# Loads of the first weights placed between those of k and v, and v in rows of 1 KB, in an attention-and-softplus kernel

## Chip, cores, metric

One core of one Trainium2 chip. The time is that of the device in microseconds (us), over whole executions of one program. The engines are PE (TensorE, matrix products), DVE (VectorE), ACT (ScalarE), POOL (GpSimd), and SP, which here only issues transfers (DMA). The granted clock is the share of its full speed that PE was given, as the profile recorded it; 1.00 is full.

## The reference, cut to what matters

```python
kv  = np.einsum('bhsd,bhse->bhde', k, v)              # b = 8, h = 8, s = 576, d = e = 64
out = np.einsum('bhsd,bhde->bhse', q, kv)
x   = out / np.sqrt(np.mean(out*out, -1, keepdims=True) + 1e-06) * g_norm   # -> (4608, 512)
h   = x @ w_in                                        # 512 -> 2048
y   = (np.maximum(h, 0) + np.log1p(np.exp(-np.abs(h)))) @ w_out             # 2048 -> 512
```

The two weights arrive as 64-bit floats.

## The kernel before

A plan written in the kernel sorts all tasks by a position number, engine by engine, and the tasks are then emitted in that order. Every engine works through its own list in order. What matters here is the start: the weights of 16 chunks (w_in and w_out each) are fetched and converted from 64-bit words into three 32-bit parts, four chunks of them for the first phase; k and v of a batch give kv, q times kv gives rows, these are normalised and turned, and then the large products begin: h from x and w_in, the sums from softplus(h) and w_out.

The conversion of a weight is a chain between ACT and DVE, in tiles of which there is one or two:

```python
f  = add("SP", 450, fetch, when, pos, [raw], size=2300, behind=int(pos) - 3)
a1 = add("ACT", 670, square, [f], pos, [sq], [raw])
a2 = add("ACT", 670, low, [f], pos, [lf], [raw])
d1 = add("DVE", 430, high1, [f], pos, [t], [raw])
d2 = add("DVE", 690, high2, [d1], pos, [], [raw])
d3 = add("DVE", 690, mask, [d2, a1], pos, [], [sq])
over_done.append(add("ACT", 910, beyond, [a1], pos, [junk], [sq, junk]))   # the overflow check
d4 = add("DVE", 430, power, [d3], pos, [p])
d5 = add("DVE", 690, rest, [d4, a2], pos, [], [lf])
ready = add("DVE", 690, total, [d3, d5], pos, [w], [t, p])
# ... then divide(): high (ACT), low (DVE), low_up (ACT), two products (PE), third (ACT)
```

k, v and q come by tiles of 128 tokens and 8 heads, so one row of a transfer is the 64 floats of a token and a head, 256 B:

```python
for b, r0, n, s0 in parts(t):
    nc.sync.dma_start(out=x[r0:r0 + n], in_=src[b, :, s0:s0 + n].rearrange("h s d -> s h d"))
# kv of a batch, for each of its tiles: four products of two heads, 128x128x128
nc.tensor.matmul(kv[:, p], lhsT=pairs(k_slots[t].tile[r0:r0 + n], p),
                 rhs=pairs(v_slots[t].tile[r0:r0 + n], p), ...)
```

and the weights' place in the plan is one number for both fetching and converting:

```python
if c < 4:
    pos = -18.0 + 0.8 * j if j < 2 else -13 + 1.6 * j     # j = 2 * chunk + (1 for w_out)
# ... later chunks at later places ...
fetched.append(weight(j, pos, ()))
```

## Time and profile before

| | before |
|---|---|
| time, median of 6 executions | 949.6 us (948.8 to 950.8) |
| profiled execution (948.7 us, as fast as the fastest of the six) | span 946.9 us, mean granted PE clock 0.996 |
| PE busy | 920.4 us, 97% |
| PE idle up to 66 us / 66 to 940 us / at the end | 21.4 / 0 / 5.2 us |

How to read it: PE runs without a gap from 66 us to 940 us, so only the first 66 us are open to a change that leaves PE's work as it is. The prediction shows the views that say so. Beside those, the page's part on transfers, with the packets by size and the time that the queue's packets took as a share of all 16 DMA engines' span:

```profile
DMA packets 172738, 135.63 MB, mean 143 GB/s; under 512 B 118656, under 2 KB 126848, under 8 KB 172672
...
q1 hardware_dynamic: 172512, 134.77, 48.3%
```

Over two thirds of all packets have under 512 B; nearly all of these are the 256 B rows of k, v and q (36 tiles of 1024 rows for each, 110592).

### The profile page before, as it was taken

Reading aid. Unit: us, or ns where it says so; the run is one execution under the profiler, and the core shown is the slowest. Engines: PE = TensorE matmul, PEld = TensorE weight load, DVE = VectorE, ACT = ScalarE, POOL = GpSimd, SP = SyncE. Lnnn points to the kernel's source line nnn. Section 1 sums busy time; section 2 is a strip of 40 time slices with the busy share of each in tenths; the row PEclk is TensorE's granted clock in tenths of the full one; section 3 lists DMA queues with packets and bytes.
Section 4 is the critical chain, followed back from the end, with each engine's and each line's share of the span. In section 5 each row is a group of like instructions: output and inputs, shape, how many; then the busy total and the mean of one; then the engine's idle time right before and its main releaser. Section 6 shows DMA issues by size and latency. Waiting matters only on the chain.

```text
span 946.9 us, 13479 instructions
## 1 busy us (share of the span) xinstructions
PE 920.4 (97%) x4978; PEld 834.2 (88%) x4978; DVE 596.5 (63%) x1043; ACT 443.7 (47%) x871; POOL 66.6 (7%) x42
## 2 busy tenths in 40 slices
PE   4889999999999999999999999999999999999997
PEld 3779999999999999998999999999999999999996
DVE  4997776867767566777676666485554544544552
ACT  4886665656656554454344334274233233233231
POOL 0213221222222000000000000000000000000000
PEclk9999999999999999999999999999999999999999
DMA  9996878777764433333333343442322332322321
GB/s 225 252 201 168 245 200 228 204 224 193 209 187 170 167 123 123 127 108 127 125 137 116 126 149 101 145 145 100 101 100 100 100 101 101 100 76 85 100 74 67
DMA packets 172738, 135.63 MB, mean 143 GB/s; under 512 B 118656, under 2 KB 126848, under 8 KB 172672
## 3 DMA queue, kind: packets, MB, share of 16 engines
q1 hardware_dynamic: 172512, 134.77, 48.3%
q8 instruction: 39, 0.64, 0.3%
q14 instruction: 27, 0.22, 0.1%
q10 hardware_dynamic: 160, 0.00, 0.0%
HBM read 93.85 MB, written 40.89 MB: 142 GB/s over the span
## 4 chain that ended last, share of the span: by engine, by line
PE 94%; DVE 2%; DMA 1%; ACT 1%; issue 0%; SPq 0%; POOL 0%; DVEq 0%; POOLq 0%
PE s L530 42%; PE h L523 42%; PE o L435 4%; PE o L461 3%; PE tp L455 2%; PE tp L477 1%; DMA kvt<-in_v_dram 1%; DVE w L289 0%; DVE t L273 0%; DVE t L268 0%; DVE p L286 0%; DMA out_dram<-qT 0%; PE s L461 0%; POOL r L469 0%; DVE r L465 0%
## 5 line engine op out<-in xcount | busy, mean ns | idle before, releaser
L530 PE MATMUL s<-w,gv 128*128 128x512 f32 x1728 | 438.5, 396 | 0.0
L523 PE MATMUL h<-xv,w 128*128 128x384 f32 x2304 | 435.9, 337 | 0.1
L523 PEld LDWEIGHTS h<-xv,w 128*128 128x128 f32 x2304 | 406.0, 188 | 14.6 <-ACT g L543 0.4
L530 PEld LDWEIGHTS s<-w,gv 128*128 128x128 f32 x1728 | 318.1, 188 | 57.9 <-issue 0.5
L543 ACT ACTIVATE g<-h 128x384 f32<-128x384 f32 x192 | 94.5, 492 | 417.0 <-PE h L523 408.7
L534 DVE TENSOR_TENSOR gv<-g,gv 128x384 fp32r<-128x384 f32 x192 | 106.7, 556 | 183.1 <-ACT gv L545 182.8
L538 DVE SCALAR_TENSOR_TENSOR gv<-gv 128x384 fp32r<-128x384 f32 x192 | 106.9, 557 | 5.2
L545 ACT ACTIVATE gv<-g 128x384 fp32r<-128x384 f32 x192 | 100.8, 525 | 6.1 <-PE s L530 1.4
L398 DVE TENSOR_TENSOR xv<-xt,xv 128x512 fp32r<-128x512 f32 x102 | 70.2, 688 | 45.0 <-ACT xv L395 44.8
L469 POOL TENSOR_TENSOR r<-r,half 128x8 f32<-128x8 f32 x36 | 65.9, 1832 | 238.6 <-DVE r L466 235.7
L401 DVE SCALAR_TENSOR_TENSOR xv<-xv 128x512 fp32r<-128x512 f32 x108 | 74.6, 691 | 2.9
L395 ACT ACTIVATE xv<-xt 128x512 fp32r<-128x512 f32 x102 | 62.9, 623 | 2.0 <-DMA xt<-x 2.0
L435 PE MATMUL o<-kvt,kvt 128*128 128x128 f32 (+1 forms) x320 | 45.7, 292 | 11.4 <-DMA kvt<-in_v_dram 11.4
L435 PEld LDWEIGHTS o<-kvt,kvt 128*128 128x128 f32 (+1 forms) x320 | 42.9, 204 | 14.9 <-issue 11.4
L570 DVE SCALAR_TENSOR_TENSOR qT<-s,scale,kvt 128x512 f32<-128x512 f32 x36 | 26.9, 749 | 37.3 <-PE s L530 29.8
L570 DVE SCALAR_TENSOR_TENSOR qT<-s,kvt 128x512 f32<-128x512 f32 x36 | 24.6, 687 | 25.5 <-PE s L530 18.1
L461 PE MATMUL o<-kv_diag,qT 128*128 128x128 f32 (+1 forms) x296 | 37.0, 276 | 0.0
L461 PEld LDWEIGHTS o<-kv_diag,qT 128*128 128x128 f32 (+1 forms) x296 | 34.6, 179 | 1.5 <-issue 0.3
L465 DVE TENSOR_REDUCE r<-x 128x8 f32<-128x512 f32 x36 | 24.6, 684 | 15.0 <-ACT x L485 14.6
L491 ACT ACTIVATE xg<-tp,g_col 128x512 f32<-128x512 f32 x36 | 24.7, 686 | 12.8 <-PE tp L477 12.3
L472 DVE TENSOR_TENSOR x<-o,r 128x512 f32<-128x512 f32 x33 | 22.7, 688 | 6.7 <-POOL r L469 6.1
L480 ACT COPY qT<-tp 128x512 f32<-128x512 f32 x36 | 21.0, 582 | 12.5 <-PE tp L455 12.2
(61 smaller groups left out, 453.5 us busy)
## 6 DMA issues: line engine op xcount, KB each, us to landing
xt<-x SPq DMA_DIRECT2D x102, 256.0 KB, 3.3
kvt<-part SPq DMA_DIRECT2D x72, 256.0 KB, 3.9
x<-xg SPq DMA_DIRECT2D x36, 256.0 KB, 2.9
part<-xg SPq DMA_DIRECT2D x36, 256.0 KB, 2.6
part<-qT SPq DMA_DIRECT2D x36, 256.0 KB, 2.3
out_dram<-qT SPq DMA_DIRECT2D x36, 256.0 KB, 2.8
raw<-in_moe_w_in_dram SPq DMA_DIRECT2D x16, 512.0 KB, 4.7
raw<-in_moe_w_out_dram SPq DMA_DIRECT2D x16, 512.0 KB, 4.7
```

The source lines that it names most:

```text
L395: nc.scalar.activation(cols(0, F32R), x.tile, func=AF.Copy, scale=DOWN)
L398: nc.vector.tensor_tensor(out=cols(1, F32R), in0=x.tile, in1=cols(0), op=ALU.subtract)
L401: nc.vector.scalar_tensor_tensor(out=cols(2, F32R), in0=cols(1), scalar=-RADIX, in1=cols(0), op0=ALU.mult, op1=ALU.add)
L435: nc.tensor.matmul(kv[:, p], lhsT=pairs(k_slots[t].tile[r0:r0 + n], p), rhs=pairs(v_slots[t].tile[r0:r0 + n], p), start=(i == 0 and p == 0 ...
L461: nc.tensor.matmul(pairs(y[r0:r0 + n], p), lhsT=qT.tile[:, p, r0:r0 + n], rhs=kv_diag[b % 2][:, p], start=(p == 0), stop=True, skip_group_ ...
L469: nc.gpsimd.tensor_tensor(out=r.tile, in0=r.tile, in1=half, op=ALU.pow)
L523: nc.tensor.matmul(hp, lhsT=w_in.tile[:, i, kd * P:(kd + 1) * P], rhs=xv.tile[:, i, kd], start=(m == 0), stop=(m == 3 * KD - 1))
L530: nc.tensor.matmul(mine[i].tile, lhsT=gv.tile[:, m, i * P:(i + 1) * P], rhs=w_out.tile[:, m], start=(c == cs[0] and m == 0), stop=(c == cs ...
L534: nc.vector.tensor_tensor(out=gv.tile[:, 1], in0=g.tile, in1=gv.tile.bitcast(F32)[:, 0], op=ALU.subtract)
L538: nc.vector.scalar_tensor_tensor(out=gv.tile[:, 2], in0=f32[:, 1], scalar=-RADIX, in1=f32[:, 0], op0=ALU.mult, op1=ALU.add)
L543: a = add("ACT", 490, lambda: nc.scalar.activation(new(g, [P, NT]), h.tile, func=AF.Softplus, scale=1.0 + E), [a], s, [g], [h])
L545: a = add("ACT", 530, lambda: nc.scalar.activation(new(gv, [P, 3, NT], F32R)[:, 0], g.tile, func=AF.Copy, scale=DOWN), [a], s, [gv])
```

## The change

Two intents. First, loads and conversions of the first phase's weights get places of their own, two separate lists of numbers, so that chunk 1's weights are loaded among batch 0's k and v, and converted while DVE and ACT would wait. Second, k and v of two heads are loaded with four neighbouring tokens per partition: the sum over tokens in kv doesn't care for their order. In v a row is then 1 KB on both sides. In k the source row is 1 KB too, but in the tile the two heads have to lie side by side for each token, so its pieces stay at 256 B and the tile takes two transfers. The core of the diff, cut (`...`):

```diff
+    P0 = [-16.0, -13.7, -11.8, -9.7, -5.1, 0.0, -13.9, 2.7, -33.5, -33.3, -24.2, -17.7, -12.2, -10.2, 15.3, -2.2, 1.5, -10.5, 6.5, 7.0, 5.0, 4.0, 4.5, 6.5]
+    CONVERT, FETCH, EARLY = P0[:8], P0[8:16], P0[16:]
...
-    rings = dict(xv=2, gv=3, g=2, raw=2, lf=1, sq=1, junk=1, t=1, p=1, w=1,
+    rings = dict(xv=2, gv=3, g=2, raw=2, lf=1, sq=2, t=1, p=1, w=1,
...
-        f = add("SP", 450, fetch, when, pos, [raw], size=2300, behind=int(pos) - 3)
+        f = add("SP", 450, fetch, (), fetch_pos, [raw], size=1800, behind=int(pos) - 3)
...
-                nc.scalar.activation(new(junk, [P, d_model], BF16), sq.tile, func=AF.Identity, scale=2.0 ** -126,
-                                     bias=big, accum_out=over[:, j:j + 1])
+                nc.scalar.activation(sq.tile, sq.tile, func=AF.Identity, scale=2.0 ** -126, bias=big,
+                                     accum_out=over[:, j:j + 1])
...
-            over_done.append(add("ACT", 910, beyond, [a1], pos, [junk], [sq, junk]))
+            over_done.append(add("ACT", 910, beyond, [d3], pos + (4 if c in PHASES[0] else 0), [], [sq]))
...
+                src = src[b, 2 * p:2 * p + 2, :MAIN].rearrange("h (s i) d -> s h i d", i=4)
+                if s is ks:
+                    for h in range(2):
+                        nc.sync.dma_start(out=x[:, h::2], in_=src[:, h])
+                else:
+                    nc.sync.dma_start(out=x.rearrange("s (h i) d -> s h i d", h=2), in_=src)
...
+                        l, r = pairs(ks.tile, i), vs.tile.rearrange("s (h i) d -> s h i d", h=2)[:, :, i]
...
-            if c < 4:
-                pos = -18.0 + 0.8 * j if j < 2 else -13 + 1.6 * j
+            if c in PHASES[0]:
+                pos = CONVERT[j]
...
-            fetched.append(weight(j, pos, ()))
+            weight(j, pos, FETCH[j] if c in PHASES[0] else pos)
```

The places of the early rows and of kv are changed a little as well (EARLY), and the sizes with which the plan reckons transfers (1200 to 900 and the like).

More of the change, by code (lines that the diff above doesn't have):

```diff
@@ L205 @@
     ORDER = [(ph, n, c) for ph, cs in enumerate(PHASES) for n in range(n_blocks) for c in cs]
-    step_of = {o: s for s, o in enumerate(ORDER)}
+    phase_of = {c: ph for ph, cs in enumerate(PHASES) for c in cs}
     first_step = {}
@@ L228, in w_source, with weight @@
         return src[:, c * n:(c + 1) * n].rearrange("(a p) f -> p a f", p=P)
-    def weight(j, pos, when):
+    def weight(j, pos, fetch_pos):
         c, of_out = divmod(j, 2)
@@ L247, in fetch @@
                 out=x.rearrange("p n w -> p (n w)").rearrange("p (a f) -> p a f", a=src.shape[1]), in_=src)
-        f = add("SP", 450, fetch, when, pos, [raw], size=2300, behind=int(pos) - 3)
+        f = add("SP", 450, fetch, (), fetch_pos, [raw], size=1800, behind=int(pos) - 3)
         if wide:
-            sq, lf, t, p, junk = (slot(n) for n in ("sq", "lf", "t", "p", "junk"))
+            sq, lf, t, p = (slot(n) for n in ("sq", "lf", "t", "p"))
             def words_of():
@@ L295, in weight @@
             d2 = add("DVE", 690, high2, [d1], pos, [], [raw])
-            d3 = add("DVE", 690, mask, [d2, a1], pos, [], [sq])
-            over_done.append(add("ACT", 910, beyond, [a1], pos, [junk], [sq, junk]))
+            d3 = add("DVE", 690, mask, [d2, a1], pos, [])
+            over_done.append(add("ACT", 910, beyond, [d3], pos + (4 if c in PHASES[0] else 0), [], [sq]))
             d4 = add("DVE", 430, power, [d3], pos, [p])
@@ L303, in weight @@
                         [f], pos, [w], [raw])
-        if c < PLACES or c in range(10, 12):
+        if c < PLACES or phase_of[c] - phase_of[c - PLACES] > 1:
             divide(j, w, ready, pos, "p", c < 4)
@@ L307, in weight @@
             spilled = dram.tile([P, d_model], F32, name=f"w_spill{j}")
-            st = add("SP", 350, lambda: nc.sync.dma_start(out=spilled, in_=w.tile), [ready], pos, [], [w], 1200)
+            st = add("SP", 350, lambda: nc.sync.dma_start(out=spilled, in_=w.tile), [ready], pos, [], [w], 900)
             again = slot("x" if of_out else "q")
@@ L311, in weight @@
             ld = add("SP", 350, lambda: nc.sync.dma_start(out=new(again, [P, d_model]), in_=spilled),
-                     [st], back, [again], [], 1200, behind=last_step[c - PLACES] - 1)
+                     [st], back, [again], [], 900, behind=last_step[c - PLACES] - 1)
             divide(j, again, ld, back, "xg")
-        return f
     def divide(j, w, ready, pos, ring, by_pe=False):
@@ L368, in parts @@
         return [(b, 0, S - s0, s0), (b + 1, S - s0, P - S + s0, 0)]
-    kv_rows = [[(t, pt[1], pt[2]) for t in range(n_tiles) for pt in parts(t) if pt[0] == b] for b in range(B)]
+    first_tile = [b * S // P for b in range(B)]
     xd = [dram.tile([P, KD * P], F32, name=f"x{t}") for t in range(n_tiles)]
@@ L380, in run @@
                 nc.sync.dma_start(out=x[r0:r0 + n], in_=src[b, :, s0:s0 + n].rearrange("h s d -> s h d"))
-        return add("SP", 700 * len(parts(t)), run, (), pos, [s], [], 1250, behind=int(pos) - 3)
+        return add("SP", 700 * len(parts(t)), run, (), pos, [s], [], 1220, behind=int(pos) - 3)
     def split(ph, t, x, ready, pos):
@@ L412 @@
     first_high = {}
-    k_slots, v_slots, k_ready = {}, {}, {}
     kv_ready = {}
@@ L419, in x_pos @@
         n = t // TB
-        return t - 12 if n == 0 else first_step[0, n] - (5 if n == 1 else 7) + t % TB
+        return t * EARLY[0] + EARLY[1] if n == 0 else first_step[0, n] - (EARLY[2] if n == 1 else EARLY[3]) + t % TB
     def kv_of(b):
-        pos = x_pos(kv_rows[b][0][0]) - (3 if b else 2)
+        pos = x_pos(first_tile[b]) - (EARLY[4] if b else EARLY[5])
         bank = slot("o")
         last = None
-        for i, (t, r0, n) in enumerate(kv_rows[b]):
-            if t not in k_slots:
-                k_slots[t], v_slots[t] = slot("kvt"), slot("kvt")
-                k_ready[t] = [load_rows(k, t, k_slots[t], pos - 2.5 + 0.5 * i), load_rows(v, t, v_slots[t], pos - 2.5 + 0.5 * i)]
-            def run(t=t, r0=r0, n=n, i=i):
-                kv = new(bank, [P, NP, P]) if i == 0 else bank.tile
-                for p in range(NP):
-                    nc.tensor.matmul(kv[:, p], lhsT=pairs(k_slots[t].tile[r0:r0 + n], p),
-                                     rhs=pairs(v_slots[t].tile[r0:r0 + n], p),
-                                     start=(i == 0 and p == 0), stop=(i == len(kv_rows[b]) - 1),
+        MAIN = 4 * P
@@ new lines, in kv_of, with load, run @@
+        for p in range(NP + 1):
+            ks, vs = slot("kvt"), slot("kvt")
+            tail = p == NP
+            n = S - MAIN if tail else P
+            def load(src, s, p=p, tail=tail, n=n, ks=ks):
+                x = new(s, [P, H, D])
+                if tail:
+                    nc.sync.dma_start(out=x[:n], in_=src[b, :, MAIN:].rearrange("h s d -> s h d"))
+                    return
+                src = src[b, 2 * p:2 * p + 2, :MAIN].rearrange("h (s i) d -> s h i d", i=4)
[4 more added lines that the diff above has]
+                    nc.sync.dma_start(out=x.rearrange("s (h i) d -> s h i d", h=2), in_=src)
+            lds = [add("SP", ns, lambda src=src, s=s, load=load: load(src, s), (), pos - EARLY[6] + 0.5 * p, [s], [],
+                       620 if tail else size, behind=int(pos - 2) - 3)
+                   for src, s, ns, size in ((k, ks, 900, 1250), (v, vs, 500, 900))]
+            def run(ks=ks, vs=vs, p=p, tail=tail, n=n):
+                kv = new(bank, [P, NP, 2, D]) if p == 0 else bank.tile
+                for i in range(4):
+                    if tail:
+                        l, r = pairs(ks.tile[:n], i), vs.tile[:n, 2 * i:2 * i + 2]
+                    else:
+                        l, r = pairs(ks.tile, i), vs.tile.rearrange("s (h i) d -> s h i d", h=2)[:, :, i]
+                    nc.tensor.matmul(kv[:, i if tail else p], lhsT=l, rhs=r, start=(p == 0 and i == 0), stop=tail,
@@ L438, in run @@
                                      skip_group_check=True)
-            last = add("PE", 820 if n == P else 1080, run, k_ready[t] + [last], pos + 0.5 * i,
-                       [bank] if i == 0 else [], [k_slots[t], v_slots[t]])
+            last = add("PE", 1080 if tail else 820, run, lds + [last], pos + 0.5 * p,
+                       [bank] if p == 0 else [], [ks, vs])
         kvd = kv_diag[b % 2]
@@ L443, in kv_of @@
         kv_ready[b] = [
-            add("ACT", 360, lambda: nc.scalar.copy(kvd[:D, :, :D], bank.tile[:D, :, :D]), [last] + old, pos + 2.5, [], [bank]),
-            add("DVE", 430, lambda: nc.vector.tensor_copy(kvd[D:, :, D:], bank.tile[D:, :, D:]), [last] + old, pos + 2.5, [], [bank])]
+            add("ACT", 360, lambda: nc.scalar.copy(kvd[:D, :, :D], bank.tile[:D, :, 0]), [last] + old, pos + 2.5, [], [bank]),
+            add("DVE", 430, lambda: nc.vector.tensor_copy(kvd[D:, :, D:], bank.tile[D:, :, 1]), [last] + old, pos + 2.5, [], [bank])]
     def rows(t):
@@ L449, in rows @@
         q_s, tp, qT, o, x, r, xp, xg = (slot(n) for n in ("q", "tp", "qT", f"s{t}" if t < TB else "o", "x", "r", "tp", "xg"))
-        ld = load_rows(q, t, q_s, pos - 3)
+        ld = load_rows(q, t, q_s, pos - EARLY[7])
         def turn_q():
@@ L493, in rows @@
         x_there[t] = add("SP", 350, lambda: nc.sync.dma_start(out=xd[t], in_=xg.tile.rearrange("p a t -> p (a t)")),
-                         [a], pos + 0.5, [], [xg], 1200)
+                         [a], pos + 0.5, [], [xg], 900)
         if t < AT_ONCE:
@@ L501, in x_again @@
         ld = add("SP", 350, lambda: nc.sync.dma_start(out=new(xt, [P, KD, P]).rearrange("p a t -> p (a t)"), in_=xd[t]),
-                 [x_there[t]], pos - 1, [xt], [], 1200, behind=first_step[ph, t // TB] - 5)
+                 [x_there[t]], pos - 1, [xt], [], 900, behind=first_step[ph, t // TB] - 5)
         split(ph, t, xt, ld, pos)
@@ L568, in leave @@
             ld = add("SP", 350, lambda: nc.sync.dma_start(out=new(pt, [P, d_model]), in_=part[ph - 1, t][0]),
-                     [part[ph - 1, t][1]], pos - 3, [pt], [], 1200, behind=int(pos) - 4)
+                     [part[ph - 1, t][1]], pos - 3, [pt], [], 900, behind=int(pos) - 4)
             a = add("DVE", 700, lambda: nc.vector.scalar_tensor_tensor(
@@ L573, in leave @@
         dst = out[t * P:(t + 1) * P] if ph == LAST else dram.tile([P, d_model], F32, name=f"part{ph}_{t}")
-        st = add("SP", 350, lambda: nc.sync.dma_start(out=dst, in_=ot.tile), [a], pos, [], [ot], 1200)
+        st = add("SP", 350, lambda: nc.sync.dma_start(out=dst, in_=ot.tile), [a], pos, [], [ot], 900)
         part[ph, t] = dst, st
@@ L601 @@
         nc.vector.memset(kvd, 0.0)
-    fetched = []
+    EACH = (first_step[PHASES[1][0]] - 9) / len(PHASES[1])
     for c in range(KF):
         for j in (2 * c, 2 * c + 1):
-            if c < 4:
-                pos = -18.0 + 0.8 * j if j < 2 else -13 + 1.6 * j
-            elif c < 10:
-                pos = 5.0 + 6.5 * (c - 4) + 3 * (j % 2)
-            else:
-                pos = first_step[10] - 64.0 + 9 * (c - 10) + 4.5 * (j % 2)
-            fetched.append(weight(j, pos, ()))
+            if c in PHASES[0]:
+                pos = CONVERT[j]
+            elif c in PHASES[1]:
+                pos = 5.0 + EACH * (c - PHASES[1][0] + 0.5 * (j % 2))
+            else:
+                pos = first_step[PHASES[2][0]] - 64.0 + 9 * (c - PHASES[2][0]) + 4.5 * (j % 2)
+            weight(j, pos, FETCH[j] if c in PHASES[0] else pos)
     for b in range(B):
@@ L623 @@
     for s in range(len(ORDER)):
-        if s == first_step[10]:
+        if s == first_step[PHASES[2][0]]:
             whole_scale(s - 4)
```

## The prediction

> **What bounds the kernel now.** I read the shares and the 40 slices of the page first, then the busy times of each engine by stretch, then who waited for whom in the first 66 us, then the timeline of the start, and the DMA rates of the first 43 us. The page's first two parts:
>
> ```profile
> PE 920.4 (97%) x4978; PEld 834.2 (88%) x4978; DVE 596.5 (63%) x1043; ACT 443.7 (47%) x871; POOL 66.6 (7%) x42
> ...
> PE   4889999999999999999999999999999999999997
> ...
> DMA  9996878777764433333333343442322332322321
> ```
>
> PE is the bound: full in all slices but the first three and the last. A change that neither removes nor shortens a PE instruction can only win PE idle time back. Where that idle lies is in the busy times by stretch (columns: the stretch and its length in us; PE, PEld, DVE, ACT, POOL busy us with counts; granted clock; DMA share; GB/s):
>
> ```profile
> 0.00:9.00 9.00, 0.02 (x1) 0.05 (x1) 5.29 (x13) 5.74 (x11) 0.70 (x6) 1.00 0.84 205
> 9.00:26.00 17.00, 12.48 (x64) 10.76 (x64) 6.93 (x13) 6.92 (x14) 0.00 (x0) 0.86 1.29 242
> 26.00:43.00 17.00, 12.60 (x87) 10.89 (x87) 15.99 (x30) 13.68 (x26) 5.53 (x3) 0.94 1.12 246
> 43.00:66.00 23.00, 19.51 (x124) 16.97 (x123) 22.26 (x41) 20.66 (x43) 3.49 (x2) 1.00 1.03 232
> 66.00:300.00 234.00, 234.00 (x1481) 214.55 (x1480) 171.03 (x311) 148.84 (x291) 54.96 (x30) 1.00 0.73 203
> ```
>
> PE idle: 9.0 + 4.5 + 4.4 + 3.5 = 21.4 us up to 66 us, none from 66 to 940, and 5.2 in the last 7. Two limits follow each other in the start. From 9 to 26 us DVE and ACT work 6.9 of 17 us while DMA is above a full share: **transfers** limit. From 26 to 66 us DVE is busy 38.3 of 40 us: **DVE** limits, with ACT (34.3) just behind. The waits of the first 66 us say for what:
>
> ```profile
> PE o L435 <- DMA kvt<-in_v_dram: 11.4, 3, 9.0
> ...
> DVE t L264 <- DMA raw<-in_moe_w_in_dram: 10.0, 2, 8.2
> ...
> PE tp L477 <- DVE x L472: 2.9, 3, 2.6
> ...
> PE h L342 <- ACT w L330: 2.8, 3, 1.3
> ```
>
> PE waits for v; DVE stands 8.2 us because the third weight (w_in of chunk 1) lands only at 22.6 us. In the timeline:
>
> ```profile
> 22.63 0.43 DVE L264 TENSOR_SCALAR t<-raw 128x512 uint32<-128x512 uint32 x1 [8.21 <-DMA raw<-in_moe_w_in_dram]
> ...
> 26.31 2.94 PE L461 MATMUL s<-kv_diag,qT 128*128 128x128 f32 x16
> ...
> 40.16 0.63 PE L477 MATMUL tp<-ident_r,x 128*128 128x128 f32 x4 [2.58 <-DVE x L472]
> ...
> 42.80 2.33 PE L523 MATMUL h<-xv,w 128*128 128x384 f32 x12
> ```
>
> So the idle DVE of 14 to 22 us is missed later, when the same conversions compete with the normalisation for DVE: PE stands 2.58 us for a DVE product, and the first large matmul starts at 42.8.
>
> **What the Trainium skill says.** "DMA: Bandwidth & Descriptors", section Specifications, gives 512 B as the smallest transfer for line rate, and section Why small descriptors are slow names a fixed cost per descriptor. The trace agrees: in the 40 slices of 0 to 43 us, those with k, v and q alone (256 B rows) hold 217 GB/s, those where weights (1 and 4 KB rows) land reach 333 to 362:
>
> ```profile
> GB/s 0 38 224 333 362 192 270 217 219 217 217 217 217 218 218 217 211 213 231 339 262 311 320 234 232 334 269 224 299 331 245 217 248 153 236 206 263 216 196 263
> ```
>
> "Perfetto Trace Analysis", section Optimization Strategy, says a kernel can have several regimes with different most-contended engines, and that interleaving them may help. The trace agrees that they are separate here, DVE at 6.9 of 17 us and then 38.3 of 40. "TensorE: Matmul & The Clock Gate", section What's actually happening, says the array runs at half rate by default and after an idle window. The trace has granted clock 0.86 from 9 to 26 us, and 16 matmuls of L461 in 2.94 us where 8 warm ones take 1.05; I count no gain from it.
>
> **The change, part by part.**
>
> 1. *v in 1 KB rows.* A 256 KB tile at 217 GB/s takes 1.21 us; at about 335 GB/s (the weights' rate; an estimate for 1 KB rows) 0.78. So 0.43 us less for each full v tile, four per batch. k reads the same tokens, but its destination stays in 256 B pieces, so it stays at 1.21 and costs a second issue (0.43 us of queue on SP, which is not the limit). PE does the same: five groups of four products per batch before and after, same shapes. The right operand is now two runs of 64 elements; I expect 275 ns as before.
>
> 2. *Order of loads.* In the changed program's order, chunk 1's w_in moves from behind the fourteenth load to the place after the second v, and its w_out to the place after the third v. My ledger: the two first weights are down at 6.4 us (the first v at 8.84, less two tiles), then 1.21 per k or q, 0.78 per v, 1.54 per weight (512 KB at 340 GB/s), half tiles 0.6. It gives first v 8.4, w_in 11.9, w_out 16.7, batch 0's last v 21.1 us. Before, the first product over that last v began at 23.27, so kv is whole **2.1 us earlier**, although a fourth weight has gone ahead of it. After the copies of kv (ACT is the later one here, near 23.8) the first product q·kv starts at about 24.4 against 26.31: **1.9 us earlier**.
>
> 3. *Conversions in the gap.* One weight is 0.43 + 0.69 + 0.69 + 0.43 + 0.69 + 0.69 = 3.6 us of DVE plus 0.68 for the low part (L326) = 4.3. Before, at 26.31, DVE has left 0.69 + 0.69 + 0.68 of the third weight and five whole ones: 2.1 + 21.5 = 23.6 us. After, following DVE's and ACT's new orders with these durations, w_in is converted from 13.1 and w_out to about 23: at 24.4 the low part of the fourth weight and four whole weights are left, 0.7 + 17.2 = 17.9. The DVE-bound stretch is **5.7 us shorter**.
>
> 4. *The overflow check (ACT, 0.71 + 0.19 us) now writes in place after the mask, at a later place.* Same work, eight of them in the start; it no longer sits between the first weights' square and low part, but needs the mask done. A few tenths either way.
>
> 5. *Later part.* Planned transfer sizes (1200 to 900 and the like) reorder issues, not work. PE had no gap from 66 to 940, with DVE at 73% and DMA share 0.73 up to 300 us: I expect no gap still.
>
> On the path: the 1.9 us of part 2 moves everything behind it forward and counts whole. Of the 5.7 us only what ends as PE idle counts. PE idle from 26 to 66 was 7.9 us. Following the new DVE order, the first large matmul starts at about 40.5 us, with a fifth weight and two more transposes of q behind it (0.85 + 1.26 us of PE work done earlier, same kernel total). So up to there PE gains 42.8 - 40.5 + 2.1 = 4.4 us. Behind it, PE had 3.5 us of gaps to 66, most of them for conversions (L342 waits 1.3 and 1.1 us at 57.3 and 52.5); with three chunks' weights ready I keep 1.5 of it, another 2.0. Sum 4.4 + 2.0 = **6.4 us** (the 1.9 is in the 4.4). 949.9 - 6.4 = **943.5 us**.
>
> **Rivals.**
> - *DVE and ACT eat the gain.* ACT was busy 34.3 of 40 us, and in my replay ACT, not DVE, holds up the low part of the third weight (about 1.5 us). If ACT's in-order queue is what limits from 15 to 40 us, the first large matmul comes at 42 or later, and only the 2 us of later gaps and some tenths are won: 947 to 949. For it: the three-engine ping-pong per weight; against it: the check is postponed for the first weights.
> - *The weights push k and v back.* If 1 KB rows run at the 217 GB/s of the small rows, four v tiles cost 1.7 us more and kv is whole at 22.8: about 945 us. Against it: w_in itself moves in 1 KB rows, and slices with it show over 330.
> - *More than I think.* If the cold clock also goes (16 products at 2.94 instead of 2.1 us, and two groups of 8 at 2.05 and 1.91 instead of 1.06), 2 to 3 us more: 940 to 941.
> - *A new wait in the first phase*, from the new order of loads, with kvt buffers held by k longer: PE would show gaps after 66 us. Against it: none there now. Slower than 950 only in this case.
>
> **Range and chances.** Idle before the first v (about 8 us) and at the end (5.2) stays, and some 4 us at least between, so the most to be won is near 14 us, 1.5%. Faster by over 2% (below 930.9) would need 19 us: 2%. Slower by over 2% needs a new stall of 19 us: 1%. Within 2%: 97%. The 80% range goes from ACT eating most of the gain to the clock gaining as well: 939.0 to 948.0.
>
> **What would show it.** The busy times of the new run: PE idle to 66 us near 15 instead of 21.4; DVE idle between 9 and 26 us down from 10.1 to about 4; the third weight's L264 successor starting near 13 us, not 22.6; the wait for v by PE after the first one gone or below 1 us; first q·kv product near 24.4 and first large matmul near 40.5; GB/s above 217 in the start. If the first large matmul stays at 42 to 43, the first rival holds; if PE shows gaps after 66 us, the last. If PE busy changes by more than 2 us in warm stretches, the strided operand costs something and my part 1 is wrong.

## The result, and the profile after

The changed kernel takes 941.95 us (median of 6 executions, 940.5 to 944.3), the kernel before 949.63 us in the same rounds. A ratio here is the mean time of one kernel's fast executions over that of the other's of the same rounds, so not quite the ratio of the medians: 0.9921, 95% interval 0.9902 to 0.9939. Executions over 1.5% slower than the fastest of the same kernel are left out of the means.

The six times lie in two groups: 940.54, 940.56 and 940.62 us with a mean granted clock of 0.998 to 0.999, and 943.29, 943.39 and 944.34 us with 0.993. The profile on hand is of the slowest, 944.34. Its first line of engines, and the busy times by stretch (columns as in the prediction):

```profile
PE 921.1 (98%) x4978; PEld 834.6 (89%) x4978; DVE 597.9 (63%) x1043; ACT 447.7 (47%) x871; POOL 66.7 (7%) x42
```

```profile
0.00:9.00 9.00, 0.04 (x1) 0.07 (x1) 5.33 (x13) 5.20 (x9) 0.70 (x6) 1.00 0.75 209
9.00:26.00 17.00, 12.88 (x57) 10.25 (x58) 12.23 (x22) 10.90 (x23) 0.00 (x0) 0.86 1.23 263
26.00:43.00 17.00, 14.18 (x92) 12.40 (x90) 14.40 (x27) 12.73 (x24) 6.24 (x4) 0.84 0.90 227
43.00:66.00 23.00, 23.00 (x161) 21.36 (x161) 19.83 (x36) 17.89 (x35) 4.62 (x4) 1.00 0.97 255
66.00:300.00 234.00, 233.68 (x1469) 213.71 (x1468) 174.57 (x316) 152.84 (x298) 54.30 (x30) 1.00 0.70 202
```

PE executes the same number of instructions (4978), in as much busy time. PE's idle time up to 66 us has fallen from 21.4 to 15.9 us, and most of that is in the last stretch: 43 to 66 us is now without a gap, where 3.5 us were idle. From 9 to 26 us DVE works 12.2 us instead of 6.9. PE's clock from 26 to 43 us, however, is 0.84 in this execution, below the 0.94 of before.

The timeline has the four events that the prediction named:

```profile
13.03 0.43 DVE L267 TENSOR_SCALAR t<-raw 128x512 uint32<-128x512 uint32 x1
...
26.40 3.78 PE L482 MATMUL s<-kv_diag,qT 128*128 128x128 f32 x16
...
40.98 0.63 PE L498 MATMUL tp<-ident_r,x 128*128 128x128 f32 x4 [1.17 <-DVE x L493]
...
44.47 2.33 PE L544 MATMUL h<-xv,w 128*128 128x384 f32 x12
```

The third weight's conversion starts at 13.03 us and waits for nothing (22.63 before). PE's longest wait for a product of the normalisation on DVE is about 1.2 us where it was 2.58. But in this execution the first product of q and kv starts at 26.40 us (26.31 before), and the first large product at 44.47 (42.80 before): later, not earlier. The gain lies behind it: PE's list reaches that product with more other work done (a fifth weight, two more transposes of q) and then runs through. And the transfers:

```profile
DMA packets 148673, 135.63 MB, mean 144 GB/s; under 512 B 86400, under 2 KB 102784, under 8 KB 148608
...
q1 hardware_dynamic: 148448, 134.78, 47.0%
```

32 full v tiles of 1024 small packets have become 32 of 256 (118656 - 32768 = 85888; the 512 beyond that would be 16 for each of the 32 added transfers of k). The queue's packet time fell from 48.3% of 946.9 us to 47.0% of 942.6, that is by 14.3 us, 0.45 us for each v tile, taken over the whole execution. Packet times overlap (their share was 1.29 from 9 to 26 us in the kernel before), so this is not elapsed time.

### The profile page after: what moved, and what is told of

Read it like the earlier page. It is cut to its first block, busy times and chain, and to the rows that moved or that the text cites. A ratio compares the mean times of both kernels' runs of the same rounds, so it can differ in the third digit from the quotient of the medians.

```text
span 942.6 us, 13502 instructions
## 1 busy us (share of the span) xinstructions
PE 921.1 (98%) x4978; PEld 834.6 (89%) x4978; DVE 597.9 (63%) x1043; ACT 447.7 (47%) x871; POOL 66.7 (7%) x42
## 4 chain that ended last, share of the span: by engine, by line
PE 96%; DMA 2%; SPq 1%; DVE 0%; ACT 0%; issue 0%; POOL 0%; DVEq 0%; POOLq 0%
PE h L544 42%; PE s L551 42%; PE o L458 4%; PE o L482 3%; PE tp L498 2%; PE tp L476 2%; DMA x<-xg 1%; DMA q<-in_q_dram 1%; DMA kvt<-in_v_dram 1%; PE s L482 0%; SPq L442 0%; DMA out_dram<-qT 0%; POOL r L490 0%; SPq L444 0%; PE h L343 0%
## 5 line engine op out<-in xcount | busy, mean ns | idle before, releaser
L482 PEld LDWEIGHTS o<-kv_diag,qT 128*128 128x128 f32 (+1 forms) x296 | 34.3, 179 | 1.2 <-issue 1.0
```

Source lines behind the costliest of these rows:

```text
L482: nc.tensor.matmul(pairs(y[r0:r0 + n], p), lhsT=qT.tile[:, p, r0:r0 + n], rhs=kv_diag[b % 2][:, p], start=(p == 0), stop=True, skip_group_ ...
```

## The experiments

Twelve kernels ran, in three calls; those of one call share a chip and the executions of the kernel before (medians 949.80, 949.80 and 949.98 us). Each was timed in five rounds.

### The changed kernel again

No edit.

> The changed kernel once more. Its six times so far lie in two groups, 940.5 to 940.6 us at a granted clock of 0.998 to 0.999 and 943.3 to 944.3 at 0.993. If the clock between 20 and 32 us makes the two groups: again two groups about 3 us apart, each with its clock, nothing between. If it is plain scatter: times spread from 940 to 944 without relation to the clock. If the profile falls into the faster group, the product of q with kv (L482) starts before 26 us and 16 of them take near 2.1 us, not 3.78.

Measured: 941.06 us median of four (940.64, 940.69, 941.43 at clock 0.997 to 0.999, and 943.24 at 0.994), ratio 0.9914 (0.99 to 0.9927). The profile is of a fast one, 940.64. Its stretches from 9 to 43 us, and from PE's timeline the two late events, with a wait for v between them:

```profile
9.00:26.00 17.00, 13.13 (x72) 10.78 (x73) 14.44 (x25) 12.77 (x25) 0.00 (x0) 0.90 1.23 268
26.00:43.00 17.00, 13.40 (x98) 11.50 (x98) 15.28 (x30) 13.95 (x27) 7.36 (x4) 1.00 1.10 267
```

```profile
24.37 2.05 PE L482 MATMUL s<-kv_diag,qT 128*128 128x128 f32 x16 [0.24 <-DVE kv_diag L466]
...
35.92 1.13 PE L458 MATMUL o<-kvt,kvt 128*128 128x128 f32 x8 [1.36 <-DMA kvt<-in_v_dram]
...
41.30 2.32 PE L544 MATMUL h<-xv,w 128*128 128x384 f32 x12
```

The same program, on the same orders: with the clock at 1.00 from 26 us on, the first products of q and kv (x16) start at 24.37 us and take 2.05, where the slower execution had 26.40 and 3.78. The first large product is 3.2 us earlier. By finer stretches the slower execution had a clock of 0.60 from 20 to 26 us and 0.50 from 26 to 30; this one had 0.72 from 14 to 20 and 1.00 from there on. So the two profiles differ by when PE's clock is low. One time of the four, 941.43, lies a little between the groups.

### The weights in their old places

```diff
-    P0 = [-16.0, -13.7, -11.8, -9.7, -5.1, 0.0, -13.9, 2.7, -33.5, -33.3, -24.2, -17.7, -12.2, -10.2, 15.3, -2.2, ...
+    P0 = [-20.5, -19.7, -12.3, -10.7, -9.1, -7.5, -5.9, -4.3, -20.5, -19.7, -12.3, -10.7, -9.1, -7.5, -5.9, -4.3, ...
```

> The changed kernel, but chunk 1's weights (and the later ones of the first phase) are fetched and converted in the places of the kernel before: behind batch 0's k, v and q. v in 1 KB rows, the check in place and the planned sizes stay as changed. Theory 1 (the gain comes from converting chunk 1's weights in the idle time of 13 to 26 us): the gain is lost for the most part, 946 to 949 us, DVE busy under 9 of the 17 us from 9 to 26, and PE again with gaps after 43 us. Theory 2 (the gain comes from the faster rows of v): 941 to 944.

Measured: 950.14 us (949.2 to 950.6), ratio 1.0004 (0.9992 to 1.0016): the whole gain is gone, more than theory 1 expected (946 to 949). Its stretches from 9 to 66 us:

```profile
9.00:26.00 17.00, 12.36 (x66) 10.85 (x67) 9.66 (x18) 9.08 (x18) 0.00 (x0) 0.89 1.19 262
26.00:43.00 17.00, 13.58 (x85) 11.43 (x84) 14.87 (x27) 14.27 (x29) 4.39 (x3) 0.91 1.08 263
43.00:66.00 23.00, 19.39 (x106) 17.50 (x107) 21.80 (x40) 18.77 (x37) 4.61 (x3) 0.85 0.59 149
```

PE has its gaps back behind 43 us (3.6 us), and its clock is lower there as well. The waits that PE has there are other ones than before the change: 2.3 us for a DVE product of the normalisation and 1.7 us for ACT's copies behind it, none for a converted weight. DVE worked 9.7 us from 9 to 26, a little more than the bound of 9, and far less than the changed kernel's 12.2. Theory 1 holds: without the placement, the 1 KB rows, the check in place and the planned sizes together are worth nothing.

### The placement without the 1 KB rows

```diff
-                src = src[b, 2 * p:2 * p + 2, :MAIN].rearrange("h (s i) d -> s h i d", i=4)
-                if s is ks: ... two transfers ... else: ...
+                nc.sync.dma_start(out=x, in_=src[b, :, p * P:(p + 1) * P].rearrange("h s d -> s h d"))
...
-                        l, r = pairs(ks.tile, i), vs.tile.rearrange("s (h i) d -> s h i d", h=2)[:, :, i]
+                    l, r = pairs(ks.tile[:n], i), vs.tile[:n, 2 * i:2 * i + 2]
```

> The changed kernel with every engine's order of work kept, but k and v loaded by token tiles in 256 B rows, each in one transfer (the tokens' order in kv as before). It takes only the 1 KB rows away. Theory 1: little is lost, 942 to 945 us (estimate: four full v tiles at 0.43 us each, 1.7 us later kv at most). Theory 2 (rows): 947 or more. It also saves one issue on SP for each k tile; if SP's issues limit the start, it can even be faster, 939 to 941.

Measured: 944.68 us (944.25 to 946.17), ratio 0.995 (0.9938 to 0.9962). This run also has one issue fewer for each k tile, and it keeps the check in place, the second `sq` tile, the planned sizes and the places of early rows and kv (EARLY). So the placement, with these, is worth about 4.7 us (0.5% of 949.8), and on top of it the rows are worth 3.4 us (0.995 over 0.9914 is 1.0036, times 941). That is twice what four tiles of batch 0 make. PE's timeline points to where the other half is, in batch 1:

```profile
39.26 0.91 PE L450 MATMUL o<-kvt,kvt 128*128 128x128 f32 x6 [1.16 <-DMA kvt<-in_v_dram]
```

The fourth tile of batch 1 is waited for, and is multiplied at 39.26 us here against 35.92 in the fast execution above. Both batches lie before the first large product, eight v tiles at 0.43 us make 3.4. But in this profile the first product of q and kv is already late by as much (27.70 us against 24.37), with a clock of 0.71 from 20 to 26 us, so this pair does not separate the batches. The pair with PE kept busy, below, does.

### The 1 KB rows without the placement

The kernel before with the new loading of k and v (the diff's part on kv), positions, check and sizes as before.

> The kernel before with the new loading of k and v alone (1 KB rows of v, k in two transfers); weights, check and positions as before. Theory 1: 947 to 950 us, DVE still idle for some 8 us before the third weight. Theory 2: 941 to 944. My ledger: batch 0's last v lands 1.7 us earlier, so at most 2 us less than before.

Measured: 952.37 us (950.12 to 953.99), ratio 1.0027 (1.0012 to 1.0041): slower than before, which neither theory expected. Two stretches:

```profile
26.00:43.00 17.00, 12.73 (x79) 11.25 (x78) 14.82 (x28) 12.49 (x24) 5.54 (x3) 0.83 0.90 223
43.00:66.00 23.00, 19.56 (x116) 17.21 (x115) 20.95 (x37) 18.90 (x39) 3.49 (x2) 0.93 0.71 178
```

PE's idle time up to 66 us is as before (21.4 us), but the clock is at 0.83 and 0.93 instead of 0.94 and 1.00, and PE's busy time over the execution is 3.1 us longer (923.5). The first product of q and kv did start earlier (25.03 us against 26.31); by the first large product that was lost (44.99 against 42.80). Why PE's gaps fall so that the clock drops is not shown; the plan gives another order of work to all engines here.

### One more transfer for each v

```diff
-                src = ....rearrange("h (s i) d -> s h i d", i=4)
+                src = ....rearrange("h (i s) d -> s h i d", i=4)
-                    nc.sync.dma_start(out=x.rearrange("s (h i) d -> s h i d", h=2), in_=src)
+                    for h in range(2):
+                        nc.sync.dma_start(out=x[:, 4 * h:4 * h + 4], in_=src[:, h])
```

> The changed kernel with tokens of a row 128 apart: v, like k, comes in 256 B rows and in two transfers of 128 KB. Same order of work on every engine. Against the run without 1 KB rows but with single transfers (944.7 us), it has one more issue for each v and each k. If only the rows' transfer time counts: 944 to 946. If issues on SP count as well (some 0.6 us each in the start): 946 to 949.

Measured: 945.85 us (944.7 to 948.9), ratio 0.9959 (0.9945 to 0.9974), against 0.995 (0.9938 to 0.9962) of the run with single transfers. The intervals overlap, so a cost of the added issues, 1 us by the medians, is not clear of noise. That the loss comes with the small rows, whatever their number of transfers, is.

### The overflow check as before

```diff
-            over_done.append(add("ACT", 910, beyond, [d3], pos + (4 if c in PHASES[0] else 0), [], [sq]))
+            over_done.append(add("ACT", 910, beyond, [a1], pos, [junk], [sq, junk]))
```

> The changed kernel with the overflow check as in the kernel before: into a junk tile, right after the square, in the weight's place. Part 4 of the prediction took it for a few tenths of a us either way: 941 to 942.5. If the check's 0.9 us of ACT per weight in the first 26 us holds conversions up: 944 to 948.

Measured: 942.92 us (940.22 to 944.49), ratio 0.9922 (0.9906 to 0.9937), that of the changed kernel being 0.9921. The check in place is worth nothing in time. (The second `sq` tile stays in this run; no run takes it away alone.)

### PE kept busy in its gaps

```diff
+    FILL = {0: 18, 3: 6, 4: 1, 6: 5, 7: 3, 11: 2}      # before which PE task, how many
     for t in plan.order():
+        if t.engine == "PE": ... FILL[...] times:
+            nc.tensor.matmul(y, lhsT=ident, rhs=ident, start=True, stop=True)
         t.run()
```

> The changed kernel with 35 small products of the identity (128x128, into an unused bank, never read) in PE's gaps before 26 us: 18 before the first product of k and v, 6, 1, 5, 3 and 2 before later ones. Nothing else is moved. If the low clock of 14 to 32 us makes the two groups of times (940.6 and 943.4 us): all executions in one group at 940 to 941, clock 0.997 or more, granted clock 1.00 from 26 to 43 us, first product of q and kv (L482) near 24.4 us in the profile. If the groups have another cause: two groups again, or all later by the products' own time (0.27 us each, up to 4 us).

Measured: 940.68, 940.76, 940.82 and 941.39 us, all at clock 0.999, ratio 0.9903 (0.989 to 0.9915). One group, at the place of the faster one:

```profile
9.00:26.00 17.00, 14.31 (x109) 12.75 (x108) 14.36 (x26) 13.00 (x26) 0.00 (x0) 1.00 1.23 273
26.00:43.00 17.00, 12.76 (x93) 10.95 (x92) 14.76 (x28) 13.26 (x26) 7.36 (x4) 1.00 1.00 253
```

With the last run below, which has the same products, that is eight of eight fast executions at a clock of 0.998 or more; without products six of the changed kernel's ten were in the faster group. So the clock is the cause of the two groups as far as these runs show, and in this kernel work that nobody reads keeps executions out of the slower one. It is not faster than the changed kernel's own good executions.

The same products in the kernel before (in seven of its gaps):

> The kernel before with the same kind of 35 small products in PE's gaps. Its eleven times in the last rounds run from 948.7 us at clock 0.997 to 951.9 at 0.991. If the clock is the cause: 947.5 to 948.7, all close together, and the change is then worth 7 to 8 us between kernels with equal clock. If not: as before, 949.8.

Measured: 951.14 us (950.26 to 952.49), ratio 1.0011 (0.9999 to 1.0023), clock 0.993 to 0.998. A miss: the clock was not held. In the profile it was 0.50 from 26 to 30 us, although two of the added products stand there, at 28.19 us; just before, at 25.16, PE had stood 2.36 us for v with no product in that gap. From 26 to 43 us the clock was 0.83, and the first large product came at 45.88 us instead of 42.80. So the kernel before couldn't be compared at an even clock this way. And the run without 1 KB rows, with the products:

> The run with k and v in 256 B rows and single transfers, with the 35 small products of warm_after, so that both are compared at one clock. warm_after took 940.8. If the 1 KB rows are worth only batch 0's four tiles at 0.43 us: 942.3 to 942.8. If batch 1's v, loaded before the first large matmul as well, counts too (eight tiles, 3.4 us): 944 to 944.8. If the clock made the difference between the two: 941 to 941.5.

Measured: 945.44 us (944.18 to 947.48), ratio 0.9953 (0.9938 to 0.9969), clock 0.993 to 1.000. Here too the products did not hold the clock in all executions. The two with the highest clock, 944.18 us at 1.000 and 944.33 at 0.997, are 3.4 to 3.5 us above the 940.8 of the kept-busy changed kernel. So the clock did not make the difference of the rows, and its size is that of eight tiles. The profiles of the two kept-busy kernels split it. First the one with 1 KB rows, then the one without, each with the first product of q and kv and with the products over the third v tile of batch 1:

```profile
24.00 2.01 PE L482 MATMUL s<-kv_diag,qT 128*128 128x128 f32 x16
...
33.16 1.13 PE L458 MATMUL o<-kvt,kvt 128*128 128x128 f32 x8 [0.56 <-issue]
```

```profile
25.59 2.01 PE L474 MATMUL s<-kv_diag,qT 128*128 128x128 f32 x16
...
36.37 2.05 PE L450 MATMUL o<-kvt,kvt 128*128 128x128 f32 x8 [1.20 <-DMA kvt<-in_v_dram]
```

Batch 0 makes 1.6 us, which is four tiles; by the third tile of batch 1 it is 3.2. From 20 to 36 us the clock was 0.96 or more in both.

### Less work for DVE

In either kernel, for the six weights of chunks 1 to 3, two of the DVE steps are left out; the plan is told nearly the same durations, so that the order hardly changes. The values lose the last bits of the weights.

```diff
-            d4 = add("DVE", 430, power, [d3], pos, [p])
-            d5 = add("DVE", 690, rest, [d4, a2], pos, [], [lf])
-            ready = add("DVE", 690, total, [d3, d5], pos, [w], [t, p])
+            if j in range(2, 8): ready = add("DVE", 1930, <t + lf in one addition>, [d3, a2], pos, [w], [t, lf])
+            else: ... as before ...
```

> A wrong result on purpose. The kernel before, with two of the DVE steps (power 0.43 us, product 0.69 us) left out for each of the six weights from chunk 1 to 3: 6.7 us less DVE work in the start, while loads, ACT and PE work stay. If DVE limits from 26 to 66 us, as the prediction has it: 4 to 6 us faster, 944 to 946, PE idle after 26 us down from 7.9 us to 2 to 4. If ACT or the arrival of the weights limits: under 1.5 us faster, 948.5 or more.

Measured: 948.42 to 949.54 us in the five fast executions, ratio 0.9991 (0.9978 to 1.0005). The profiled execution took 3568 us, and says nothing here. So 6.7 us less for DVE won nothing that can be told from noise. Their clocks were low, though, 0.992 to 0.993, where the kernel before ranges from 0.991 to 0.998. Its three executions at 0.993 took 949.99 to 950.07 us, the three of this run 948.42 to 948.91. They were run at other times. At equal clock the cut is thus worth some 1.1 to 1.6 us, far less than the 4 to 6 expected: DVE alone does not limit the start of the kernel before.

> A wrong result on purpose. The same six weights with two DVE steps less, in the changed kernel. If the change has taken DVE off the path (transfers of k, v and q, and the chain of the normalisation, bound PE's first 43 us): under 1.5 us faster, 940 to 942. If DVE still limits: 3 us or more, below 938.5.

Measured: 942.25 us (940.49 to 944.38), ratio 0.992 (0.9905 to 0.9936), clock 0.995 to 0.997, no faster than the changed kernel. Neither kernel's start is bound by DVE alone.

### A try at more

```diff
-    ... -24.2, -17.7, -12.2, -10.2, ...      # in FETCH, on top of the kept-busy version
+    ... -24.2, -17.7, -11.1, -9.4, ...
```

> A try at a faster version: warm_after, with the loads of chunk 2's weights moved from places -12.2 and -10.2 to -11.1 and -9.4, so that one k and v tile more of batch 1 goes ahead of each. Batch 1's v was waited for 1.4 us at 35.9 us. If that wait is on the path: 939.5 to 940.3. If chunk 2's conversion then comes too late for the third large matmul: 941.5 to 943.

Measured: 941.74 to 942.31 us in four executions at clock 0.998 (a fifth: 1016.7 us at 0.851, the profiled one), ratio 0.9918 (0.9903 to 0.9932): 1.3 us more than the version it started from, not clear of its 0.9903 (0.989 to 0.9915). The gain did not come; the times lie where the second expectation put them, but the only profile is the slow one, so its reason is not shown. No version beat the changed kernel's good executions.

## Why the prediction was right or wrong

The time, 943.5 us predicted and 941.95 measured, lay in the range, 6.4 us of gain against 7.7 by the medians. No execution took 941.95: the median falls between the two groups. The sum was 4.4 us up to the first large product and 2.0 behind it. By the same reckoning the fast profile has 42.80 - 41.30 + 2.1 = 3.6 us and 3.5 behind it, the slow one 42.80 - 44.47 + 2.1 = 0.4 and 3.5. So the near hit is partly luck: the first term was too large, by much at the low clock, and the second too small, and both leaned on DVE as the limit, which did not hold (below). By steps:

**PE is the bound, and only its gaps up to 66 us can be won.** Right but for the clock: in the slow profile PE's busy time is the same within 0.7 us, and between 66 us and the end 0.3 us are idle. In the fast one it is 3.2 us less (917.2), with the same instructions.

**1 KB rows save 0.43 us a tile.** Right: 1.6 us for the four tiles of batch 0 in the kept-busy pair, 0.40 each, and 0.45 by the queue's packet time. But the sum counted them for batch 0 alone. Batch 1's tiles are on the path to the first large product too, and with them the rows are worth 3.4 us, given the placement. That term had half of its size; without the placement they are worth nothing.

**The ledger of the loads.** Right for the weights (conversion predicted from 13.1 us and to about 23; it started at 13.03 and ended at 23.26). The first product of q and kv was predicted at 24.4 us and the first large one at 40.5: in the fast profile they came at 24.37 and 41.30, in the slow one at 26.40 and 44.47. The last v of batch 0 was reckoned to be down at 21.1 us; its products began at 22.24 in the fast profile, behind other work of PE and not behind the transfer. A wait for v of 1.36 us stayed in batch 1, where the prediction named none or less than 1 us.

**The DVE-bound stretch is 5.7 us shorter.** What was seen was right, the reason not. DVE did convert two weights in the gap, and putting them back costs everything. But the sentence "From 26 to 66 us DVE is busy 38.3 of 40 us: DVE limits, with ACT (34.3) just behind" took occupancy for the limit. Taking 6.7 us from DVE left the time at 0.9991 of before, 1.1 to 1.6 us less at equal clock. What the placement moves forward is the whole conversion, ACT's part (in the kernel before 0.67 + 0.67 + 0.71 + 0.19 + 0.63 + 0.63 + 0.60 = 4.1 us a weight) as well as DVE's. In the kernel before, PE's waits of 43 to 66 us, in the view by who waited for whom, were all for ACT's outputs in that chain:

```profile
PE h L342 <- ACT w L330: 2.4, 2, 1.3
PE h L341 <- ACT w L323: 0.8, 1, 0.8
```

After, that view has no wait at all for this stretch. One step further back the trace does not decide: L330 at 51.81 and 56.60 us started within 0.05 us of the end of the DVE step that it needs (L326), with ACT itself at work right up to it, and L323 at 54.79 had waited 0.40 us for DVE. Late arrival is out as the cause there: the two waits of DVE for raw words were both before 23 us. Whether ACT's in-order list, ACT and DVE in turn, or the back and forth of the chain through single tiles is the limit, no run tells apart; it stays open. A run with less work for ACT, or for both engines, was not made; with 6.7 us less, DVE would have some 32 us of work in those 40 (an estimate: 38.3 less most of the 6.7), less than ACT's 34.3.

**No gain from the clock.** Wrong in size. The prediction put 2 to 3 us for it among the rivals ("More than I think", 940 to 941 us), and half of the executions do just that. An account from the first 66 us of six profiles, my own arithmetic: PE idle time, plus what the clock withholds ((1 - clock) times the stretch), against the span.

| profile | PE idle to 66 us | withheld to 66 us | sum, against before | span, against before |
|---|---|---|---|---|
| before | 21.4 | 3.4 | | 946.9 |
| changed, low clock | 15.9 | 5.1 | -3.8 | -4.3 |
| changed, high clock | 16.4 | 1.7 | -6.7 | -8.1 |
| placement alone | 15.8 | 3.4 | -5.6 | -4.4 |
| 1 KB rows, old places | 20.7 | 6.9 | +2.8 | +1.5 |
| 1 KB rows alone | 21.4 | 6.7 | +3.3 | +3.1 |

The two terms together follow the spans within 1.5 us. The placement takes the gaps away, the clock decides how much of it an execution gets, and the rows alone only move the gaps to where the clock falls.

**The check in place, and the later part.** Right: 0.9922 with the old check, and no new wait in the later part.

**The rivals.** That ACT eats the gain did not come true: its sign, the first large product at 42 us or later, came in the slow profile (44.47), but by the clock and with the gain kept. Still, in the kernel before ACT's outputs are what PE waited for from 43 to 66 us. That the weights push k and v back did not either: the products over batch 0's last v began at 22.24 us (fast) and 23.35 (slow) against 23.27 before. Without the 1 KB rows they began at 24.65, at a lower clock than the fast one.

## What to carry to other kernels

Where a start goes through two limits in turn, transfers first and conversions after, fetch what the second needs among the transfers of the first, even ahead of data that seem more urgent; here the new places, with two weights of chunk 1 at their core, were worth 4.7 us of 949.8. Wider rows in a saturated queue pay only once the engines can use what arrives earlier: 3.4 us with the placement, nothing without. Before an engine with 95% busy time is called the limit, take work from it and see, at equal clock; and when executions of one program fall in groups, look at the granted clock before explaining a difference of less than 1%.

## What the Trainium skill lacked or had wrong

- "Perfetto Trace Analysis", section Identifying the Most-Contended Engine, has the limit of DVE and ACT read from their occupancy. DVE was busy 38.3 of 40 us here, and 6.7 us less work for it gave 0.9991 of the time (0.9978 to 1.0005), 1.1 to 1.6 us less at equal clock. The section says nothing of two engines that alternate in one chain.
- "TensorE: Matmul & The Clock Gate", section What's actually happening, calls the ramp less than 1% of a typical span, and varying from run to run. Both agree with the runs: 943.4 against 940.6 us, 0.3%. It lacks that this splits one program's executions in two groups that lie a third of the measured change apart, and that a few products in the gaps end it in one kernel (clock 0.999 in 4 of 4) and not in two others (0.993 to 0.998, and 0.993 to 1.000).
- "DMA: Bandwidth & Descriptors", section Why small descriptors are slow, gives no time for a whole tile of small rows. 256 KB in rows of 256 B against 1 KB differed by 0.45 us of packet time over the whole execution, and by 0.40 us of elapsed time in the start, where small rows alone move 217 GB/s.
- No page has whole executions of one core like the two slow ones: 3568 us at a recorded clock of 1.0, with PE busy for 3551 us where the same instructions otherwise take 920, and 1016.7 us at 0.851, of kernels that otherwise took 949 and 942 us.
